# A buffer pool closed early for two more loads in flight, and the order of a first stretch dealt anew

## The chip, the cores and the metric

The kernel runs on one NeuronCore of a Trainium2 chip. A core has five engines with instruction streams of their own: TensorE (PE in the profile, its weight load is PEld), VectorE (DVE), ScalarE (ACT), GpSimd (POOL) and SyncE (SP, which here issues most DMAs). They meet through semaphores. The DMA engines move data between HBM and SBUF; matrix products are summed in PSUM. The metric is the device time of one execution in microseconds (us).

## The reference

Eight batches of block-recurrent cross attention: 512 tokens and 32 states, 8 heads of 64. Tokens read the states, states read the tokens. The two results are put in one sequence of 544 rows per batch and 512 columns (heads side by side), in all 4352 rows, and a SwiGLU layer with RMS norm follows.

```python
scores = scale * np.matmul(x, state.transpose(0, 1, 3, 2))     # 8 x 8 x 512 x 32
a = softmax(scores);   xread = np.matmul(a, state)
scores2 = scale * np.matmul(state, x.transpose(0, 1, 3, 2))    # 8 x 8 x 32 x 512
a2 = softmax(scores2); sread = np.matmul(a2, x)
x = bridge(concat([xread, sread], axis=2))                     # 4352 x 512
xn = x / sqrt(mean(x * x) + 1e-06) * rms_g
g, val = xn @ w_gate, xn @ w_val                               # 512 x 1536 each
return silu(g) * val @ w_out                                   # 1536 x 512
```

The weights arrive as 64-bit floats. The kernel reads them as 8-byte words and makes 32-bit floats of them on the chip.

## The kernel before

**Weights.** The three matrices are cut into 18 pieces of 1 MB: piece 0 is a gate piece, 1 a value piece, 2 an output piece, and so on in threes, one three for each of six blocks of the hidden layer (in the order 0, 3, 1, 4, 2, 5). A piece is loaded as raw words into one of three buffers of the pool `raws` (L241), ScalarE makes the exponent from one 16-bit part of each word in two steps, `lin` (L274) and `ex` (L277), VectorE shifts the rest (L298) and joins the two (L302). When VectorE has joined a piece, its buffer is free, and the load of the piece three further on is issued (`load_piece(k + RAW_AHEAD)`). After each value piece the block's pair of weights is stored to HBM for later batches (`w_d`, L307); they come back in `w_m` (L222).

**The work of a batch.** The tokens' read of the states is turned round: the states are multiplied with the gate and value weights first (`own_weights`, L753; ScalarE copies the result to `v`, L765), and the hidden layer is then the product of attention weights `aT_s` and `v`. For batch 0, this is done head on (L806, silu `t` L812, product `hb` L816). Its output projection is made in groups: of a 2 by 2 split of the matrices, four products per group (L1039), some with sums of `hb` or of the output weights `wo` (`group`). Four of a group's seven go one after the other into one and the same bank of PSUM (`groups_chained`, stream `p`); each time VectorE (ScalarE in the first group) adds the bank, as it then stands, to one of four sums (`chained_sums`, stream `x`, L1078 in the profile's line for the add). Three have banks of their own (`groups_direct`, `r`). From batch 1 on, the hidden layer is made with seven products of half the size for eight (L910), with sums of `aT_s` on GpSimd (`aT_t`, L828 to L830) and of `v`, and the projection likewise on two levels (L1273). For that, VectorE makes sums of the output weights once: `wt` (L1115) and `w` with further `wt` (L1227), for outer products 2, 3 and 6 during batch 0 (stream `Q`) and 0, 1, 4 and 5 during batch 1 (stream `q`). The operands `h` of the inner products are also made on VectorE (L1321 to L1327). The states' rows of all batches go through the layer at the end.

**The order.** Nothing is scheduled by a planner on the chip. The program is cut into streams of steps, each named by a letter, and strings tell which stream takes its next step: ORDER for batch 0 and the first stretch, FIRST for batch 1, PERIOD for batches 2 to 6, LAST for batch 7, STATES for the end. Each engine then runs its own instructions in that order; a wait on one holds up what stands behind it on the same engine. Letters that matter here: `e` exponents and `d` joins of the pieces, `v` own weights, `h`, `t`, `u` hidden layer of batch 0, `s` and `S` states' reads of batches 0 and 1, `w` the first steps of batch 1, `z` a product on ones that keeps TensorE awake.

**Room.** What belongs to the attention of batch 0 and to the conversion of weights lives in pools of an exit stack `early`: `raws`, `line`, `v_0`, `conv` and `x_0`, the last with the tokens of batch 0, their scores and the like. All are closed together, when the first `k` or `w` step comes.

## Time and profile before

| what | value |
|---|---|
| median of 3 runs | 735.96 us (734.49 to 736.7) |
| profiled execution | 735.84 us |
| its span in the trace | 734.1 us |
| TensorE busy | 727.0 us (99%) |
| VectorE busy | 573.6 us (78%) |
| ScalarE busy | 350.8 us (48%) |
| GpSimd busy | 287.5 us (39%) |
| granted TensorE clock, mean | 1.00 |

The span runs from the first to the last instruction of the trace; the execution's own time is 1.74 us longer. Rows of the timeline give the start in the span, the length, engine, line, operation, output and inputs, shapes and how many instructions are put together; in brackets stands the engine's idle time just before them, and what ended it. Starts and lengths are in us. Rows of the chain give the start, the length and what the end of the run hung on at that time. A 32-bit product of four matmuls in the program stands as eight in the trace.

### The profile page before, as it was taken

The page shows a single profiled execution, that of the slowest core. Times are in us where ns is not written, and L with a number is a line of the kernel's source. Part 1 is how long each engine was busy: PE and PEld are TensorE (multiplying, and loading weights), DVE is VectorE, ACT ScalarE, POOL GpSimd, SP SyncE. Part 2 cuts the span into 40 slices and gives each one's busy share as a digit, 9 for nine tenths or more (in the row PEclk, how much of TensorE's full clock was granted, in tenths as well). Part 3 has the DMA queues.
Part 4 walks back from the last instruction along what each step waited for, and adds up shares of the span by engine and source line. Part 5 has one row for each costly group of instructions (what it writes and reads, how often), then busy time and mean ns, then how long its engine had stood idle before and what let it go on. Part 6 is the DMA issues. An engine that isn't in the chain of part 4 may idle for free.

```text
span 734.1 us, 14464 instructions
## 1 busy us (share of the span) xinstructions
PE 727.0 (99%) x5676; PEld 605.3 (82%) x5676; DVE 573.6 (78%) x972; ACT 350.8 (48%) x610; POOL 287.5 (39%) x376
## 2 busy tenths in 40 slices
PE   8999999999999999999999999999999999999998
PEld 7654657789977997799888987899779987899996
DVE  5886799999848995699569984899569955888852
ACT  5987842562365336553365326533655336411220
POOL 2322037432474128512753247412851277325400
PEclk9999999999999999999999999999999999999999
DMA  8899966973692298408870588229840782063411
GB/s 234 306 327 327 335 225 213 304 303 100 212 308 68 103 325 322 114 31 306 273 249 5 213 273 318 58 99 325 325 113 32 302 277 77 1 233 113 140 48 29
DMA packets 58940, 146.17 MB, mean 199 GB/s; under 512 B 10228, under 2 KB 30200, under 8 KB 51960
## 3 DMA queue, kind: packets, MB, share of 16 engines
q1 hardware_dynamic: 47824, 126.30, 48.6%
q10 hardware_dynamic: 11048, 18.95, 8.9%
q8 instruction: 45, 0.74, 0.4%
q14 instruction: 23, 0.19, 0.1%
HBM read 116.46 MB, written 28.77 MB: 198 GB/s over the span
## 4 chain that ended last, share of the span: by engine, by line
PE 92%; DMA 3%; DVE 2%; ACT 2%; issue 0%; SPq 0%; DVEq 0%; ACTq 0%
PE f L910 40%; PE f L1273 32%; PE pv L753 4%; PE f L1039 4%; PE pv L806 3%; PE f L1135 2%; PE at L753 2%; DMA raw<-in_moe_w_val_dram 1%; PE at L456 1%; DMA raw<-in_moe_w_out_dram 1%; DMA raw<-in_moe_w_gate_dram 1%; PE f L680 1%; PE at L374 1%; ACT ex L277 1%; ACT lin L274 1%; PE at L325 0%
## 5 line engine op out<-in xcount | busy, mean ns | idle before, releaser
L910 PE MATMUL f<-aT_s,v 128*128 128x256 f32 x504 | 120.5, 382 | 0.0
L910 PEld LDWEIGHTS f<-aT_s,v 128*128 128x128 f32 x504 | 94.4, 190 | 24.6 <-issue 7.5
L1301 POOL TENSOR_TENSOR kept<-kept 128x256 f32<-128x256 f32 x28 | 20.8, 743 | 211.5 <-DVE kept L1313 147.9
L973 DVE TENSOR_TENSOR g<-g,f 128x512 f32<-128x512 f32 x84 | 56.9, 684 | 57.6 <-PE f L910 41.3
L910 PE MATMUL f<-aT_t,vs 128*128 128x256 f32 x336 | 86.5, 381 | 0.0
L1273 PE MATMUL f<-w,h 128*128 128x128 f32 x588 | 74.4, 276 | 0.0
L1273 PEld LDWEIGHTS f<-w,h 128*128 128x128 f32 x588 | 69.7, 192 | 4.1 <-DVE eB L662 4.1
L910 PEld LDWEIGHTS f<-aT_t,vs 128*128 128x128 f32 x336 | 63.0, 190 | 10.3 <-issue 1.0
L964 ACT ACTIVATE hb<-g 128x1024 f32<-128x1024 f32 x42 | 44.4, 1058 | 54.9 <-DVE g L973 54.7
L780 POOL TENSOR_TENSOR vs<-v 128x256 f32<-128x256 f32 x42 | 31.2, 744 | 81.5 <-ACT v L765 81.4
L1286 ACT COPY kept<-f 128x512 f32<-128x512 f32 (+1 forms) x56 | 29.2, 532 | 67.3 <-PE f L1273 61.8
L765 ACT COPY v<-pv 128x512 f32<-128x512 f32 x56 | 31.1, 592 | 36.7 <-PE pv L753 34.2
L973 DVE TENSOR_TENSOR c<-c,f 128x512 f32<-128x512 f32 (+1 forms) x48 | 31.3, 652 | 17.4 <-PE f L910 17.2
L986 DVE TENSOR_TENSOR hb<-hb,f 128x512 f32<-128x512 f32 (+1 forms) x48 | 31.1, 648 | 17.5 <-PE f L910 17.5
L910 PE MATMUL f<-aT_s,vs 128*128 128x256 f32 x168 | 43.1, 379 | 0.0
L910 PE MATMUL f<-aT_t,v 128*128 128x256 f32 x168 | 43.1, 379 | 0.0
L1273 PE MATMUL f<-wo,h 128*128 128x128 f32 x336 | 42.1, 275 | 0.0
L1273 PE MATMUL f<-wo,hb 128*128 128x128 f32 x336 | 42.1, 275 | 0.0
L806 PE MATMUL pv<-aT_s,v 128*128 128x512 f32 x88 | 40.4, 599 | 0.4 <-ACT v L765 0.4
L1273 PEld LDWEIGHTS f<-wo,hb 128*128 128x128 f32 x336 | 40.3, 192 | 0.4
L1273 PEld LDWEIGHTS f<-wo,h 128*128 128x128 f32 x336 | 39.8, 192 | 0.0
L986 DVE TENSOR_TENSOR hb<-hb,c 128x512 f32<-128x512 f32 (+1 forms) x48 | 33.3, 694 | 6.1 <-ACT hb L964 5.4
(261 smaller groups left out, 1632.4 us busy)
## 6 DMA issues: line engine op xcount, KB each, us to landing
w_m<-w_d SPq DMA_DIRECT2D x48, 1024.0 KB
w<-t_d SPq DMA_DIRECT2D x49, 576.0 KB
out_dram<-kept SPq DMA_DIRECT2D x30, 256.0 KB
raw<-in_moe_w_val_dram SPq DMA_DIRECT2D x6, 1024.0 KB
raw<-in_moe_w_out_dram SPq DMA_DIRECT2D x6, 1024.0 KB
w_d<-w_m SPq DMA_DIRECT2D x6, 1024.0 KB
x_b<-in_x_dram SPq DMA_DIRECT2D x6, 1024.0 KB
x_d<-xB ACTq DMA_DIRECT2D x6, 1024.0 KB
```

The source lines that it names most:

```text
L753: TE.matmul(out=pv[e][Ns * j:Ns * j + Ns, :], lhsT=stT_g[b][D * e:D * e + D, j, :], rhs=w[D * e:D * e + D, j].rearrange("p m k f -> p (m k ...
L765: SE.copy(v[:, e].rearrange("p m k f -> p (m k f)"), pv[e])
L780: GE.tensor_tensor(out=vs[:, 0], in0=a21, in1=a22, op=ALU.add)
L806: TE.matmul(out=to[0], lhsT=lhs(i, k), rhs=r, start=(i == 0), stop=(i == len(rhs) - 1))
L910: TE.matmul(out=ps[:, i, 0:half], lhsT=l[:, i, :], rhs=r, start=(start and i == 0 and k == 0), stop=(k == len(lhs) - 1), skip_group_check= ...
L964: SE.activation(out=hb[:, 2 * mp:2 * mp + 2, 0:n].rearrange("p m (c t) -> p m c t", c=2), in_=q["g"][:, :, :, 0:half], func=ACTF.Silu if s ...
L973: VE.tensor_tensor(out=to, in0=to, in1=q[ps][:, :, 0:half], op=ALU.add)
L986: VE.tensor_tensor(out=part, in0=part, in1=val, op=ALU.mult)
L1039: TE.matmul(out=bank[:, r, :], lhsT=lhs[:, k, P * r:P * r + P], rhs=rhs[:, k], start=(start and r == 0 and k == 0), stop=(stop and k == 1) ...
L1273: TE.matmul(out=to[half][:, slot, :], lhsT=lhs[:, k, :], rhs=rhs[:, k, :], start=(fresh and n in (0, 4) and k == 0), stop=(k == QM - 1), s ...
L1286: SE.copy(of_half(k, i), banks[name][i])
L1301: GE.tensor_tensor(out=k[:, 4:8:3], in0=k[:, 5:6].to_broadcast([P, 2, QD]), in1=k[:, 4:8:3], op=ALU.add)
```

## The change

The pool `x_0` moves to an exit stack of its own, `first`. A new stream `o` of one step closes it and opens in its place a pool `raws_2` with two more buffers for raw pieces, and loads pieces 11 and 12 into them. From piece 8 on, a joined piece issues the load five further on rather than three. The two strings ORDER (397 letters, now 398) and FIRST (324, as before) are dealt anew, with the same number of steps of every stream beside the one `o`; PERIOD, LAST and STATES are unchanged.

```diff
+RAW_MORE = 2
+MORE_FROM = 8
...
 ORDER = (
-    "zzzzaazaaggaaaaaziiezzeebzgaddaabbadedbbageadbbbsssbzaaeaAAassAAsbbbbsaaaaaAAbbb"
...
+    "zzzzaazagaaaaggaazzdzbzaageeeabbeabbbaadddebbsssbzaaaaAAAAessbbbAAssdabaaabbabsd"
...
 FIRST = (
-    "vxlhthtaahhqaathhvvaahhauuuxxhtqqqththhuuthhfqhqqxqaauuuhxtuuxthqqthhtuaaqhuuqqh"
...
+    "aaaahhvattvaxxxhtvhhhhhauutttuhhhxhxtaahhqqqqqauuuutfquuxqqqhqqqtthhthhhhhuxxuuu"
...
     conv = early.enter_context(tc.tile_pool(name="conv", bufs=2))
-    x_0 = early.enter_context(tc.tile_pool(name="x_0", bufs=1))
+    first = ExitStack()
+    x_0 = first.enter_context(tc.tile_pool(name="x_0", bufs=1))
...
-        raw[k] = raws.tile([P, 8 * P + 1, 4], I16, name="raw")
+        j = k - MORE_FROM - RAW_AHEAD
+        pool = more[0] if j >= 0 and j % (RAW_AHEAD + RAW_MORE) < RAW_MORE else raws
+        raw[k] = pool.tile([P, 8 * P + 1, 4], I16, name="raw")
...
+    more = []
+
+    def more_room():
+
+        first.close()
+        more.append(early.enter_context(tc.tile_pool(name="raws_2", bufs=RAW_MORE)))
+        for j in range(RAW_MORE):
+            load_piece(MORE_FROM + RAW_AHEAD + j)
+        yield
...
-                    load_piece(k + RAW_AHEAD)
+                    load_piece(k + RAW_AHEAD + (RAW_MORE if k >= MORE_FROM else 0))
...
-               "e": exponents(), "d": values(),
+               "e": exponents(), "d": values(), "o": more_room(),
```

On SyncE, in the middle of the first stretch, where the loads of raw pieces (`raw`) stand among the stores of weight pairs (`w_d`) and a load of a pair back (`w_m`), the rows before are these; the first is piece 10 of the 18, counted from 0:

```order
L241 DMA raw_646<-in_moe_w_val_dram 128x4x1024
L307 DMA w_d1_144<-w_m_574 128x2048
L241 DMA raw_700<-in_moe_w_out_dram 128x2x2048
L241 DMA raw_743<-in_moe_w_gate_dram 128x4x1024
L241 DMA raw_747<-in_moe_w_val_dram 128x4x1024
L307 DMA w_d4_147<-w_m_714 128x2048
L222 DMA w_m_770<-w_d0_143 128x2048
L241 DMA raw_776<-in_moe_w_out_dram 128x2x2048
```

And now:

```order
L246 DMA raw_637<-in_moe_w_val_dram 128x4x1024
L322 DMA w_d1_144<-w_m_601 128x2048
L246 DMA raw_721<-in_moe_w_out_dram 128x2x2048
L246 DMA raw_723<-in_moe_w_gate_dram 128x4x1024
L246 DMA raw_741<-in_moe_w_val_dram 128x4x1024
L246 DMA raw_751<-in_moe_w_out_dram 128x2x2048
L246 DMA raw_755<-in_moe_w_gate_dram 128x4x1024
L322 DMA w_d4_147<-w_m_748 128x2048
L225 DMA w_m_777<-w_d0_143 128x2048
```

Two loads of raw pieces more stand ahead of the store of the next pair. (Line numbers in the body are 15 higher in the changed kernel, a few less near its top.)

On ScalarE, at about the same place, `lin` and `ex` are the two steps of a piece's exponents, `t` a silu of batch 0's hidden layer, `kept` and `c` the first group's sums, `v` the copies of own weights. Before:

```order
L274 ACTIVATE lin<-raw,bounds 128x1024
L277 ACTIVATE ex<-lin,bounds 128x1024
L812 ACTIVATE t<-pv 128x512
L1076 COPY kept<-f 128x512
L765 COPY v<-at 128x512 x2
```

And now, where the same `kept` and `v` stand:

```order
L827 ACTIVATE t<-pv 128x512
L1091 COPY kept<-f 128x512
L780 COPY v<-at 128x512 x2
L827 ACTIVATE t<-pv 128x512
L289 ACTIVATE lin<-raw,bounds 128x1024
L292 ACTIVATE ex<-lin,bounds 128x1024
```

The read of a piece that stood ahead of `t`, `kept` and `v` now follows them, behind a further `t`.

On TensorE, at the passage from batch 0 to batch 1, the products into the one bank (f_525 before, f_496 now) of a later group, among the own weights of batch 1 (`at`, `pv` from `w_m`) and the products with banks of their own, stood so before:

```order
L753 MATMUL at_1144<-w_m_889,stT_g_708 32x512
L1039 MATMUL f_525<-wo_153,hb_154 128x256 x4
L1039 MATMUL f_650<-wo_153,group_1106 128x256 x4
L1039 MATMUL f_651<-group_962,hb_154 128x256 x4
L1039 MATMUL f_525<-group_962,group_1106 128x256 x4
L707 MATMUL at_1203<-ident_110,sr_1060 128x128
```

And now:

```order
L768 MATMUL at_1149<-w_m_918,stT_g_702 32x512
L1054 MATMUL f_496<-wo_153,hb_154 128x256 x4
L1054 MATMUL f_627<-wo_153,group_1092 128x256 x2
L722 MATMUL at_1170<-ident_110,sr_1055 128x128
L1054 MATMUL f_628<-group_955,hb_154 128x256 x2
L1054 MATMUL f_496<-group_955,group_1092 128x256 x4
L1054 MATMUL f_628<-group_955,hb_154 128x256 x2
```

Between the two products into the one bank eight matmuls stood; now four and a transpose (`at_1170`).

On VectorE, the adds from that bank (`kept` or `c22` with f_525 or f_496) stand among the sums of weights. Before:

```order
L1078 TENSOR_TENSOR kept_637<-kept_637,f_525 128x512
L1115 TENSOR_TENSOR wt_1043<-wo_153,wt_1043 128x512
L1083 TENSOR_TENSOR c22_638<-c22_638,f_649 128x512
L1227 TENSOR_TENSOR w2_1115<-wt_1043,w2_1115 128x384 x2
L1227 TENSOR_TENSOR wt_1043<-wt_1043 128x3x128
L1078 TENSOR_TENSOR c22_639<-c22_639,f_525 128x512
```

And now:

```order
L1093 TENSOR_TENSOR kept_663<-kept_663,f_496 128x512
L1242 TENSOR_TENSOR w2_1163<-wt_1007 128x384
L1242 TENSOR_TENSOR w2_1163<-wt_1007,w2_1163 128x384
L1098 TENSOR_TENSOR c22_664<-c22_664,f_626 128x512
L1242 TENSOR_TENSOR w2_1163<-wt_1007,w2_1163 128x384
L1242 TENSOR_TENSOR wt_1007<-wt_1007 128x3x128
L1093 TENSOR_TENSOR c22_665<-c22_665,f_496 128x512
```

Between the two adds from the bank one subtraction of 128x384 more stands now, and the addition to `wt` (L1115 before) has gone ahead of the first of them.

More of the change, by code (lines that the diff above doesn't have):

```diff
@@ L27 @@
 ORDER = (
-    "zzzzaazaaggaaaaaziiezzeebzgaddaabbadedbbageadbbbsssbzaaeaAAassAAsbbbbsaaaaaAAbbb"
-    "sAdAAbbAbbdaeabvedvAbbvhhhdehteeAAAeAAudddsspteviupAvSiesvsdddhteeessshhheuxdddr"
-    "vtuTTrAevTTSWveWppxeeAAAddrrWWAAAdArppxheStppeeeddddhuhtvhdWWWxuvAveeAhthudddeAs"
-    "sehthuAAdprpSAAAAATrTrxTTppeexddvvvppxAAASSSSSSerrhheedddetupWepxerhddtWdWWWhvvv"
-    "pSkkuhAthhStAAphkkkrQkkQAAAQQxuurrTTTTppQAwwwwwwwxpprrrrkcQQQxpkpQQcQxcwQwcSS"
+    "zzzzaazagaaaaggaazzdzbzaageeeabbeabbbaadddebbsssbzaaaaAAAAessbbbAAssdabaaabbabsd"
+    "AAdAAebbbbbaevvaAbvhebhhteeAAddAeupshAsdddtuvpvvesAASsshehdSSsddhehtueeedsrWtddW"
+    "vurTTAAAvvxeiiiihAeppTTrrSAxeAAAssWoSeeppxehddWrrdddddtuppxvvvhtSAAhuheedAhhhtud"
+    "eeAAtSSSruTTpTWSpxeWTArApAAWdpxrredddeWrpAedAvpAAvveexhteeehdhAAWpuddhddedvtvvWW"
+    "ukpxWShShhkkkrtuAkkkAAhQtuTpTTTrrQpxQQArppAwwwwkxwwpQQprSwwcrQQxppkcQQQSxrcwcQ"
 )
@@ L42 @@
 FIRST = (
-    "vxlhthtaahhqaathhvvaahhauuuxxhtqqqththhuuthhfqhqqxqaauuuhxtuuxthqqthhtuaaqhuuqqh"
-    "hhqqqtuuxththhtxaxuutvxhhtxkaaxhtaakkukuahhhhuuthhhuuutttauhffaahtauuuuhuhuhutaa"
-    "apphuuGuukppappppfpkkGppppacGckkkpkkkppkpppppppckgpkkakkaakaaskkkkkpkkpascsakkaa"
-    "aagpspgsagpcsaoopgkggppkcpppppppaappppsssakoppaakkpkkpksokoopafapwwsxxxwxxxcssls"
-    "fcoo"
+    "aaaahhvattvaxxxhtvhhhhhauutttuhhhxhxtaahhqqqqqauuuutfquuxqqqhqqqtthhthhhhhuxxuuu"
+    "hatthqqxuukthktkhhuutfavqhtukaaGaqhtxxxaaffhhhuuuthhhuuutuathtuaahhtsuuuhhuuhupa"
+    "pthappcapppcpGuuukkukkkkkaakkkpppkaGppppppppcpppkkgpskpkkkkppkcgpscpggaapppksscl"
+    "pgaaakaapgkssaakkkkakppakaappppsspsspppaaaooakpogpkpckkakkppaopawwxofwxxlfcooxxx"
+    "osss"
 )
```

## The prediction

> **What bounds the kernel now.** I read the engine shares first, then busy time by stretch, then TensorE's timeline around its few holes, then the chain of work that ended last. In the shares (busy us, share of the span) TensorE has almost no room.
>
> ```profile
> span 734.1 us, 14464 instructions
> PE 727.0 (99%) x5676; PEld 605.3 (82%) x5676; DVE 573.6 (78%) x972; ACT 350.8 (48%) x610; POOL 287.5 (39%) x376
> ```
>
> 734.1 − 727.0 leaves 7.1 us without a matmul. The view by stretches (length, busy time of PE, its weight load, DVE, ACT, POOL, then clock, DMA share, GB/s) splits them:
>
> ```profile
> 0.00:82.00 82.00, 78.55 (x485) 49.73 (x486) 61.17 (x114) 65.94 (x91) 21.57 (x45) 1.00 0.90 299
> 82.00:730.40 648.40, 648.40 (x5193) 555.55 (x5191) 512.41 (x859) 284.47 (x519) 265.93 (x331) 1.00 0.54 187
> 730.40:734.10 3.70, 0.02 (x1) 0.00 (x0) 0.00 (x0) 0.37 (x1) 0.00 (x0) 0.93 0.16 44
> 1.05 0.79 PE L1413 MATMUL f<-wake 128*128 128x256 f32 x1 [1.05 <-DVE wake L160]
> ```
>
> The tail of 3.7 us is the last store, which the change does not touch, and the first 1.05 us precede any matmul. That leaves 82.00 − 78.55 − 1.05 = 2.40 us of visible waiting, all of it before 82 us. From there to the last matmul TensorE never shows idle, at full granted clock. Since the change neither adds nor removes a matmul, removing waits can pay at most about these 2.4 us, which is 0.33%; and the 650 us behind them can only lose. Something near 0.3% is also what a measurement of this kernel can tell from no change.
>
> Of the visible holes (what ended each stands in the brackets) these are the first, the largest, and the products ahead of the largest and of a small one:
>
> ```profile
> 11.96 0.63 PE L528 MATMUL at<-ident,x_b 128*128 128x128 f32 x4 [0.75 <-DMA x_b<-in_x_dram]
> 65.25 1.98 PE L806 MATMUL pv<-aT_s,v 128*128 128x512 f32 x4
> 67.65 3.70 PE L806 MATMUL pv<-aT_s,v 128*128 128x512 f32 x8 [0.42 <-ACT v L765]
> 80.26 0.81 PE L1039 MATMUL f<-wo,hb 128*128 128x256 f32 x3
> 81.16 1.10 PE L1039 MATMUL f<-group 128*128 128x256 f32 x4
> ```
>
> Matmuls' ends are modelled, so idle time understates a wait; start to start is sharper. Back to back, four products of batch 0's hidden layer and eight of its projection each take 1.72 us here:
>
> ```profile
> 57.26 1.88 PE L806 MATMUL pv<-aT_s,v 128*128 128x512 f32 x4
> 58.98 1.89 PE L1039 MATMUL f<-group 128*128 128x256 f32 x8
> 60.70 3.60 PE L806 MATMUL pv<-aT_s,v 128*128 128x512 f32 x8
> ```
>
> So the hole at 67.65 costs more than its 0.42 (65.25 + 1.72 = 66.97, some 0.1 for the change of form: 0.58), and the one at 81.16 is 81.16 − 80.26 − 3 × 0.215 = 0.25. With smaller ones, an estimate of 0.2, about 1.0 us of waiting lies between the weight product at 49.09 and batch 1's at 114.07.
>
> **What the change does to the first stretch.** The chain and ScalarE's timeline show what the pieces of weights cost:
>
> ```profile
> 36.63 8.53 DMA raw<-in_moe_w_val_dram
> 47.72 1.23 DVE L302 TENSOR_TENSOR w_m<-raw,ex 128x1024 int32<-128x1024 int32 x1 [0.36 <-ACT ex L277]
> 56.08 7.52 DMA raw<-in_moe_w_out_dram
> 63.69 1.29 ACT L274 ACTIVATE lin<-raw,bounds 128x1024 f32<-128x1024 int16 x1 [1.53 <-DMA raw<-in_moe_w_out_dram]
> 66.06 0.58 ACT L812 ACTIVATE t<-pv 128x512 f32<-128x512 f32 x1
> 67.00 1.08 ACT L765 COPY v<-at 128x512 f32<-128x512 f32 x2
> 49.09 1.09 PE L753 MATMUL at<-w_m,stT_g 64*32 64x512 f32 x16
> ```
>
> The first row is piece 7, the second its words on VectorE, the third piece 11. Piece 7 lands at 45.16 and its words are put together by 48.95, when the product at 49.09 can go. Piece 11 is issued only at 56.08 (a buffer must come free), lands at 63.6, and ScalarE stands 1.53 us in front of it. Behind that read, in ScalarE's order, are the silu `t` and the two copies `v` on which TensorE waits at 67.65. This is the hole of 0.58.
>
> *Two more buffers.* SyncE's queue now issues pieces 11 and 12 as soon as the states of batch 0 are read, behind the store of `w_d[3]`, at about 49.5, and piece 13 after piece 8's last words rather than piece 10's. The issues themselves are of equal number; SyncE's row is the store, the other the stretch behind it:
>
> ```profile
> 49.39 0.50 SPq L307 DMA_DIRECT2D w_d<-w_m  x1
> 48.00:60.00 12.00, 11.99 (x62) 8.57 (x61) 11.72 (x20) 11.57 (x15) 0.00 (x0) 1.00 0.97 326
> ```
>
> The transfers have little room to come sooner: the DMA engines are 0.97 busy from 48 to 60 us. A queue that is full moves the same bytes in the same time, so I give piece 11 one to two microseconds, not the seven by which its issue moves, and only the later pieces five or more. TensorE waits for none of the later ones. The two new issues also wait for the last reader of the pool that is given up; behind them on SyncE stands only piece 13, so a late release would delay loads, and costs the path nothing up to the seven microseconds they are ahead.
>
> *ScalarE's order.* What takes the hole at 67.65 away is mostly that the new order puts `t` and `v` ahead of the read of piece 11; 0.58, 0.25 and the small ones go together. I take the whole 1.0 us. Its lower bound is nothing (rival C).
>
> *Before 49 us.* The first part of the order is dealt anew as well.
>
> ```profile
> 23.25 0.69 DVE L580 TENSOR_TENSOR eS<-aT_s,pv 128x512 f32<-128x512 f32 x1
> 23.86 1.22 DVE L302 TENSOR_TENSOR w_m<-raw,ex 128x1024 int32<-128x1024 int32 x1
> 25.14 0.37 SPq L241 DMA_DIRECT2D raw<-in_moe_w_val_dram  x1
> 35.38 1.24 DVE w_m L302
> ```
>
> The third weight product, at 49.09, hangs on piece 7, which could be issued at 36.63 when piece 4's words at 35.38 were done, and piece 4 was issued at 25.14, behind piece 1's words. In the new order VectorE has more of batch 0's state reads behind it by then, so piece 1's words are free of one such step of 0.6 us (`eS` at 23.25). An estimate is that piece 4 gains 0.5 and the third product 0.4 us, as the copies on ScalarE between them keep their lengths. It can't be more than the visible holes ahead of that product, 2.40 − 0.42 = 2.0, and a new wait of the same size, +0.4, isn't excluded either.
>
> **What it does behind 81 us.** Here nothing can be won and the question is which cover goes. Batch 0's projection runs four products per group; two of them (first and last here) go into one bank of PSUM, and VectorE must add the first to its sum before the last may write:
>
> ```profile
> 114.07 1.09 PE L753 MATMUL pv<-w_m,stT_g 64*32 64x512 f32 x16
> 115.95 1.99 PE L1039 MATMUL f<-wo,hb 128*128 128x256 f32 x8
> 117.78 1.89 PE L1039 MATMUL f<-wo,group 128*128 128x256 f32 x8
> 121.23 1.03 PE L1039 MATMUL f<-group 128*128 128x256 f32 x4
> ```
>
> The first of the two is through issuing at 115.95 + 1.72 = 117.7, the last starts at 121.23; two other products stand between, 117.78 to 121.2, 3.45 us. In the new order half of each and a transpose stand there: 8 × 0.215 + 0.11 = 1.84 us. On VectorE the add has as much in front of it as before:
>
> ```profile
> 116.07 0.67 DVE L1083 TENSOR_TENSOR c<-c,f 128x512 f32<-128x512 f32 x1
> 118.14 1.08 DVE L1227 TENSOR_TENSOR wt<-wt 128x384 f32<-128x384 f32 x1
> 119.14 0.68 DVE L1078 TENSOR_TENSOR c<-c,f 128x512 f32<-128x512 f32 x1
> 108.11 0.55 DVE L1227 TENSOR_TENSOR wt<-wt 128x384 f32<-128x384 f32 x1
> 115.68 1.06 POOL L829 TENSOR_TENSOR aT_t<-aT_s,aT_t 128x256 f32<-128x256 f32 x1
> ```
>
> That add ended at 119.8 before, with 1.4 us to spare. I take the add to end at 119.8 to 120.2 again (one subtraction more stands ahead of it, one addition of weights less), while TensorE, early by 1.4 us and with less in between, stands ready at about 119.1: a wait of about 0.75 us. The ends: nothing, if VectorE's subtractions run at 0.55 instead of 1.08 us, and 1.1 if all run slowly. I take 0.75, since GpSimd works beside them now as before. The rows themselves show that price: the same 128x384 subtraction takes 0.55 us at 108.11, and 1.08 at 118.14 while GpSimd is adding.
>
> The Trainium skill, page "SBUF — State Buffer", section "Who interferes with whom", has a rule for it: a VectorE instruction whose two inputs are both in SBUF contends with a GpSimd instruction that reads SBUF, and the loser stands still; with one SBUF input it does not. The trace agrees: `c<-c,f`, with one input in PSUM, stays at 0.67 beside GpSimd. By the rule the wait comes to 0.75 to 1.1 us; were it wrong here, to nothing. It speaks against this change, which leaves less time for those subtractions beside GpSimd.
>
> *Batch 1's hidden layer and projection.* FIRST has the same steps in a new order; the sixteen weight subtractions stand later in it. VectorE is what TensorE can come to wait for:
>
> ```profile
> 113.00:129.00 16.00, 16.00 (x110) 11.65 (x109) 15.35 (x24) 4.57 (x9) 13.74 (x14) 1.00 0.72 246
> 130.00:190.00 60.00, 60.00 (x438) 52.32 (x423) 58.72 (x102) 31.23 (x53) 17.85 (x20) 1.00 0.65 226
> 180.14 0.49 DVE L1323 TENSOR_TENSOR h<-h,hs 128x384 f32<-128x384 f32 x1
> 180.96 1.50 PE L1273 MATMUL f<-w,h 128*128 128x128 f32 x12
> ```
>
> VectorE is idle for 1.28 us of the 60, and the operand of the product at 180.96 was ready at 180.63: 0.33 us. TensorE arriving up to 1.4 us earlier, less the 0.75 it has already waited, leaves 0.65 against 0.33 here; 0 to 0.5 us of new waiting, of which I take 0.2. The period of batches 2 to 7, the last batch and the states' own layer keep their orders, so nothing is counted there.
>
> **Sum.** −0.4 (before 49) − 1.0 (49 to 114) + 0.75 (the shared bank) + 0.2 (batch 1) = −0.45 us. The profiled execution took 735.84 (0.12 under the median of 735.96, which is well within what the three runs spread over): 735.4 us.
>
> **Rivals.**
>
> *A: all holes go and no new one opens.* VectorE's subtractions are quick and the bank is free in time. 735.84 − 1.4 = 734.4. For it: the next wait is only 0.75 us, from a time walked by hand. Against: 3.45 us between the products fall to 1.84.
>
> *B, slower: VectorE becomes the bound at the passage into batch 1.* The place is 113 to 190 us. If nine of the sixteen subtractions of weights, now later, fall beside GpSimd's work, each costs 1.08 − 0.55 = 0.53 more, 4.8 us. VectorE's 0.33 of margin and 1.28 of idle take 1.6, and beyond that point each microsecond is TensorE's: +3.2. 735.84 − 1.4 + 0.75 + 3.2 = 738.4. For it: VectorE is 98% busy there (58.72 of 60), and GpSimd works for 13.74 of the 16 us at the passage. Against: from 130 on GpSimd is busy for 17.85 of 60 only.
>
> *C: the change doesn't do what it says.* The DMA engines are full, so pieces 11 and 12 land when they did; ScalarE's reads then stand where they stood, and the 1.0 us stays: 735.84 − 0.4 + 0.95 = 736.4. For it: the share of 0.97. Against: the order itself has `t` and `v` ahead of the read of piece 11.
>
> **Chances.** Forecast 0.52, A 0.16, B 0.22, C 0.10. The limits of 0.3% are 733.8 and 738.2. A passes the lower one only if it also finds most of the holes before 49 us, 0.06; B passes the upper with 0.20, the rest of it stops short. So faster 0.06, same 0.74, slower 0.20. The range is 733.9 (A with half a microsecond more) to 738.6 (B with 0.2 more), which leaves out about 2 in 10.
>
> **What would show it.** The load of piece 11 issued near 49.5 and landing at 61 to 63; batch 0's `v` ready without a hole near 67; TensorE's weight product of batch 1 near 112.7, not 114.07; a hole of about 0.75 us ahead of the second product of the shared bank near 120, ended by VectorE's add; VectorE's idle time in 130 to 190 near nothing. It would be wrong if holes of more than 1 us ahead of `h` or `hb` appear in batch 1 (B), if the third weight product waits longer than now, or if the DMA engines deliver pieces 8 to 10 later because 11 and 12 take their share.

## The result

The changed kernel takes 733.6 us (median of 9 runs, 732.23 to 734.23), the kernel before in the runs beside it 735.7 us (9 runs, 734.49 to 736.83). The ratio is 0.9969, with a 95% interval of 0.9958 to 0.9979: 2.1 us or 0.3% faster. A second measurement gave the same ratio (0.9959 to 0.9979). I had forecast 735.4 us, in a range that began at 733.9: the sign is right, the size is not, and the time lies 0.3 us outside the range.

The page of the changed kernel, engine shares first, and the three stretches cut as those of before (the middle one ends with the last matmul):

```profile
span 731.9 us, 14461 instructions
PE 725.5 (99%) x5676; PEld 605.5 (83%) x5676; DVE 575.6 (79%) x972; ACT 348.4 (48%) x608; POOL 291.4 (40%) x376
```

```profile
0.00:82.00 82.00, 79.54 (x504) 52.89 (x505) 63.51 (x116) 66.55 (x94) 25.53 (x45) 1.00 0.88 310
82.00:728.20 646.20, 645.85 (x5174) 552.66 (x5172) 512.08 (x857) 281.47 (x515) 265.91 (x331) 1.00 0.53 187
728.20:731.90 3.70, 0.07 (x1) 0.00 (x0) 0.00 (x0) 0.37 (x1) 0.00 (x0) 0.79 0.16 45
130.00:190.00 60.00, 60.00 (x424) 53.61 (x423) 59.06 (x104) 30.62 (x52) 15.63 (x18) 1.00 0.64 227
```

The span is 2.2 us shorter. TensorE's idle time went from 7.1 to 731.9 − 725.5 = 6.4 us, which is 0.7. The other 1.5 us were *busy* time before, for the same 5676 matmuls: waits that the modelled ends of matmuls had covered. My ceiling of 2.4 us, taken from visible idle time, was therefore a ceiling for the wrong thing; that the gain stays under it is chance. The last row shows that batch 1 did not get a new bound: VectorE is busier (59.06 of 60, against 58.72), and TensorE is still never idle.

The idle time of TensorE that is left in the first 130 us, gaps under 0.15 us aside, with what ended it (the last row comes after 82 us and is new):

```profile
1.05 3.78 PE L1428 MATMUL f<-wake 128*128 128x256 f32 x8 [1.05 <-DVE wake L163]
18.58 0.63 PE L570 MATMUL at<-ident,eS 128*128 128x128 f32 x4 [0.62 <-DVE stT L354]
22.97 1.05 PE L600 MATMUL f<-of_head,eS 128*128 128x4 f32 x8 [0.30 <-DVE eS L595]
47.49 1.09 PE L768 MATMUL at<-w_m,stT_g 64*32 64x512 f32 x16 [0.36 <-DVE w_m L317]
125.30 1.58 PE L768 MATMUL pv<-w_m,stT_g 64*32 64x512 f32 x16 [0.35 <-ACT v L780]
```

The holes at 67.65 (copies `v`) and 81.16 are gone, and so are those at 36.75 and 39.19 that before had between its first and third weight product. The third weight product starts at 47.49 instead of 49.09.

**An account of lost time.** Since idle time understates waits, I add up from the trace, for all matmuls in order, the distance from one start to the next, less what that shape takes back to back (the lower quartile of its distances over the whole of before: 0.215 us for 128x256, 0.43 for 128x512). What is left is time lost, including the fixed cost of going from one shape to another. Read at the same amount of finished work instead of the same time, it can be compared between kernels whose steps have another order. The four stages are: up to 22 us of work (a little behind the first weight product), 22 to 35 (to just ahead of the third), 35 to 95 (through the passage into batch 1), and the rest.

| kernel (one profile each) | to 22 | 22 to 35 | 35 to 95 | rest | ratio to before, 95% interval |
|---|---|---|---|---|---|
| before | 10.11 | 2.95 | 10.27 | 56.58 | 1 |
| changed | 8.92 | 2.19 | 9.12 | 57.53 | 0.9969 (0.9958 to 0.9979) |
| changed, second profile | 9.36 | 2.18 | 8.87 | 56.87 | 0.9969 (0.9959 to 0.9979) |
| e1_buffers_only | 11.47 | 3.20 | 8.63 | 56.70 | 0.9986 (0.9977 to 0.9995) |
| e2_orders_only | 9.18 | 2.18 | 12.53 | 57.70 | 1.0007 (0.9998 to 1.0017) |
| e5_new_start | 9.49 | 3.13 | 9.08 | 56.59 | 0.9988 (0.9978 to 0.9998) |
| e6_old_start | 9.59 | 2.16 | 9.30 | 56.63 | 0.9982 (0.9973 to 0.9991) |
| e3_old_first | 9.47 | 2.22 | 8.88 | 57.09 | 0.9982 (0.9973 to 0.9991) |
| e4_new_first | 11.56 | 3.19 | 10.04 | 56.84 | 1.0005 (0.9997 to 1.0014) |
| e7_start_buffers | 9.33 | 3.23 | 9.06 | 56.70 | 0.9980 (0.9971 to 0.9989) |
| e8_copies_first | 9.75 | 2.16 | 8.88 | 56.64 | 0.9971 (0.9960 to 0.9982) |
| e9_softmax_first | 10.24 | 3.33 | 9.71 | 56.58 | 0.9998 (0.9989 to 1.0006) |
| e10_best | 9.13 | 2.17 | 8.85 | 56.62 | 0.9963 (0.9951 to 0.9975) |
| e11_copies_first | 10.10 | 2.85 | 12.32 | 56.73 | 1.0020 (1.0011 to 1.0030) |
| e12_join_behind | 10.17 | 3.23 | 8.46 | 56.57 | 0.9995 (0.9987 to 1.0004) |
| e13_middle_only | 9.91 | 2.18 | 10.36 | 56.75 | 1.0002 (0.9993 to 1.0011) |

Two columns are worth a look before the experiments. The second is nearly a constant of the order: 2.16 to 2.22 in the eight profiles with the new order there, 2.95 to 3.33 in the seven with the old one unaltered. The first and third scatter by a microsecond among kernels that are alike there, so a single profile settles nothing in them that is smaller. In two profiles, those of e1 and e4, the first column (11.47 and 11.56) holds something else besides: the granted TensorE clock was 0.50 between 16 and 18 us, as in no other profile here. These two are left out of means of that column.

### The profile page after: what moved, and what is told of

Its sections match the earlier page's. It is cut to its first block, busy times and chain, and to the rows that moved or that the text cites. A ratio compares the mean times of both kernels' runs of the same rounds, so it can differ in the third digit from the quotient of the medians.

```text
span 731.9 us, 14461 instructions
## 1 busy us (share of the span) xinstructions
PE 725.5 (99%) x5676; PEld 605.5 (83%) x5676; DVE 575.6 (79%) x972; ACT 348.4 (48%) x608; POOL 291.4 (40%) x376
## 4 chain that ended last, share of the span: by engine, by line
PE 94%; DMA 2%; DVE 2%; ACT 1%; issue 0%; ACTq 0%; DVEq 0%
PE f L925 40%; PE f L1288 32%; PE pv L821 4%; PE pv L768 4%; PE f L1054 3%; PE f L1150 2%; PE at L768 2%; DMA out_dram<-c 1%; DMA raw<-in_moe_w_val_dram 1%; PE f L1428 1%; PE at L471 1%; PE f L695 1%; PE at L389 1%; PE pv L550 1%; ACT ex L292 0%
## 5 line engine op out<-in xcount | busy, mean ns | idle before, releaser
L796 POOL TENSOR_TENSOR vs<-vs,v 128x256 f32<-128x256 f32 x42 | 35.8, 853 | 3.3
```

The lines of the kernel that those rows point to most:

```text
L796: GE.tensor_tensor(out=vs[:, 1], in0=vs[:, 0], in1=a11, op=ALU.subtract)
```

## Experiments: buffers and orders apart

**e1_buffers_only.** The buffers and loads of the change, with the orders of before and one letter.

```diff
-    ...hhheuxdddrvtu...
+    ...hhheuxdddorvtu...
```

> The kernel before with the two more buffers alone: its own two orders, and one step that gives up the first pool and loads pieces 11 and 12 as soon as piece 7 is joined; from piece 8 on loads run five ahead. Theory 1 (the gain is made by the orders: about half ahead of the first weight product of batch 0, the rest by the places of ScalarE's steps up to 75 us): no change, 735.7 us, within 0.5, although piece 11 lands earlier; the hole at 67.65 shrinks at most by 0.5 us. Theory 2 (the gain is made by the buffers): about 734 us. Theory 3 (half of the gain is the luck of the first transfers, which landed earlier in the profile of after although issued alike): 735.7 us as well.

Measured: 734.11 us, ratio 0.9986. The interval excludes one, so theory 1 in its pure form falls: the buffers alone gain about 1 us. Where they gain it can be seen beside e4, which has the old first stretch without the buffers (its own result stands below). In both profiles the clock fell to 0.50 for a while, TensorE lost some 1.4 us more there than in before, and the transfers did not come later by as much; so each is the other's control. The clock is the third figure from the end in the first row; three rows of e1 follow, and three of e4:

```profile
16.00:18.00 2.00, 2.00 (x34) 0.82 (x33) 1.80 (x6) 0.28 (x1) 0.00 (x0) 0.50 1.04 230
51.90 0.56 SPq L246 DMA_DIRECT2D raw<-in_moe_w_out_dram  x1
64.54 1.28 ACT L289 ACTIVATE lin<-raw,bounds 128x1024 f32<-128x1024 int16 x1 [0.91 <-DMA raw<-in_moe_w_out_dram]
66.64 3.84 PE L821 MATMUL pv<-aT_s,v 128*128 128x512 f32 x8
57.49 0.37 SPq L241 DMA_DIRECT2D raw<-in_moe_w_out_dram  x1
64.57 1.27 ACT L274 ACTIVATE lin<-raw,bounds 128x1024 f32<-128x1024 int16 x1 [0.96 <-DMA raw<-in_moe_w_out_dram]
66.71 5.51 PE L806 MATMUL pv<-aT_s,v 128*128 128x512 f32 x12
```

The hole at the copies `v` is gone in both, with the buffers and without. Piece 11 was issued at 51.90 in e1 and at 57.49 in e4, 5.6 us apart, and ScalarE, which waited for it both times, read it at 64.54 and 64.57. For this piece the buffers gained nothing; the hole is gone because TensorE came later. In e7, which has the buffers, the old order here and the full clock, it is there again (below).

What the buffers do gain stands ten microseconds further on, at piece 13. The first four rows are of before, the last is of e1:

```profile
72.98 1.27 ACT L274 ACTIVATE lin<-raw,bounds 128x1024 f32<-128x1024 int16 x1 [2.06 <-DMA raw<-in_moe_w_val_dram]
75.94 0.69 DVE L816 TENSOR_TENSOR hb<-t,pv 128x512 f32<-128x512 f32 x1 [0.81 <-ACT t L812]
77.27 0.71 DVE L450 STREAM_TRANSPOSE aT_s<-eS 128x512 f32<-128x512 f32 x1
77.42 1.27 PE L456 MATMUL at<-aT_s,rows 32*64 32x512 f32 x5
71.65 1.23 ACT L289 ACTIVATE lin<-raw,bounds 128x1024 f32<-128x1024 int16 x1
```

ScalarE waits 2.06 us for the piece; the silu `t` behind it comes late, VectorE's `hb` waits 0.81 us for `t`, and behind `hb` on VectorE stands `aT_s`, ready at 77.98, for which TensorE's products from 77.42 on wait. From 60 to 75 us of work before loses 3.2 us, e9 (a wait of 1.85 us for the piece) 3.0 and e4 (2.58) 3.8. In e5 and e12 the piece landed sooner (1.11 and 0.69), and they lose 2.3. So do e1 and e7: with the buffers the piece is issued some 7 us sooner than in e4 and e5, and ScalarE doesn't wait for it.

**e2_orders_only.** Both new orders, the `o` left out, loads three ahead throughout.

> The two new orders without the buffers: the one step that gives up the pool is left out and loads run three ahead throughout. Theory 1: most of the gain stays, 733.6 to 734.2 us. Theory 2: the gain goes, 735 us or more, with holes on TensorE ended by ScalarE's copies or by weights near 60 to 85 us, where pieces 11 to 15 come later than the new order counts on. Theory 3: near 734.6 us whichever order stands at the start.

Measured: 736.16 us, ratio 1.0007. The gain is gone, as theory 2 says: without the buffers the new orders lose 3.4 us more between 35 and 95 us of work than with them (12.53 against 9.12). The holes stand where the last pieces are used:

```profile
95.83 1.09 PE L753 MATMUL at<-w_m,stT_g 64*32 64x512 f32 x16 [1.70 <-DVE w_m L302]
99.29 0.93 PE L680 MATMUL at<-x_b,e 128*32 128x64 f32 x51 [1.31 <-ACT v L765]
85.49 10.07 DMA raw<-in_moe_w_out_dram
95.64 1.46 ACT lin L274
```

The last two rows, of the chain, tell why: a piece that is issued at 85.49, when a buffer comes free, and used at 95.6 on ScalarE, with the copies `v` behind it. Near 64 us, where ScalarE's copies `v` now stand ahead of the read of piece 11 (63.15 and 65.51), TensorE has no hole: the new order closes that one without the buffers. Neither theory 1 nor theory 2 holds alone: the new order is only good with the buffers, and the buffers pay also without it.

**e5_new_start and e6_old_start.** The first has the new order for its first 93 letters only, behind it the old one, without buffers; the second is the changed kernel with the old order for its first 95 letters. Letters that the first part has used are left out of the second, and steps that it lacks (`iia` in e5) come directly behind it, so no step is lost.

```diff
 e5_new_start
-    "zzzzaazaaggaaaaaziiezzeebzg...sAdAAbbAbbdaeabvedvAbb...
+    "zzzzaazagaaaaggaazzdzbzaage...AAdAAebbbbbaeiiavdvAbb...
 e6_old_start
-    "zzzzaazagaaaaggaazzdzbzaage...AAdAAebbbbbaevvaAbvhebhh...
+    "zzzzaazaaggaaaaaziiezzeebzg...sAdAAbbAbbdaeabevvAbvhebhh...
```

> The kernel before with the new order up to the first weight product of batch 0 only (the first 93 steps), behind it the old order, no buffers, old order of batch 1. Theory 1: first weight product near 24.7 us instead of 25.7, time 734.7 us (half of the gain). Theory 2: 735.7 us. Theory 3: the first product stands where the first transfers put it, 24.7 or 25.7 us, and the median of the runs is that of before, 735.7 us.

> The changed kernel with the old order up to the first weight product of batch 0 (95 steps), all else as changed, buffers included. Theory 1: first weight product near 25.7 us, time 734.6 us (the other half of the gain stays). Theory 2: 733.6 us. Theory 3: 733.6 us, with the first product at 24.7 or 25.7 us by luck.

Measured: 0.9988 and 0.9982. The start is worth 0.12%, or 0.9 us, where it is added to before, and 0.13%, about 1 us, where it is taken from the changed kernel. That is what theory 1 forecast for it, and it speaks against theory 3, though not strongly: e5's interval just excludes one, and e6's overlaps that of the changed kernel. The first weight product began at 24.83 and 25.17 us, where 24.7 and 25.7 were expected. Luck is there all the same: the transposes of the second half's tokens, which wait for `x_b` where it lands late, begin between 10.8 and 12.0 us in the profiles, with its load issued at 4.23 to 4.25 in all of them. It strikes old and new starts alike, and it is in the first column. At equal landing the traces give the start less: 9.75 in e8 (transposes at 11.95, new start) against 10.11 in before (11.96, old), and 9.36 in the changed kernel's second profile (11.49) against 9.59 in e6 (11.51).

**e7_start_buffers.** New start and buffers, the rest of both orders old.

```diff
-    ...ssbzaaeaAAassAAs... (ORDER up to the first v: old)
+    ...ssbzaaaaAAAAessb... (ORDER up to the first v: new; one o behind piece 7's join)
```

> The kernel before with the new start (up to the first weight product) and the two buffers, but the old order of the rest and of batch 1. If the parts add: the start gave 0.12% and the buffers alone 0.14%, so a ratio of 0.9974, and the new dealing between 25 and 125 us is worth only the 0.05% that are left to the changed kernel's 0.9969. If the buffers' gain and the start's are the same waits, seen twice: 0.9986. If it is the middle of the order that uses the buffers: 0.9986 as well, with the holes near 37 and 39 us (weights, copies of v) still there.

Measured: 0.9980. The parts may add (0.9974 was worked out, the interval is 0.9971 to 0.9989, and the buffers alone had 0.9986). The difference to 0.9969, about 0.8 us, would be the new deal's behind the start; the intervals overlap, but the table's second column shows a like amount at its place, 3.23 here and 2.19 in the changed kernel. The hole at the copies `v` is here in spite of the buffers; ScalarE waited 1.44 us for piece 11, issued at 49.23 and read at 62.88, where e5 without buffers issued it at 55.40 and read it at 62.96:

```profile
66.85 3.70 PE L821 MATMUL pv<-aT_s,v 128*128 128x512 f32 x8 [0.34 <-ACT v L780]
```

**e3_old_first and e4_new_first.** Batch 1's order old in the changed kernel, and new in the kernel before.

```diff
 FIRST = (
-    "aaaahhvattvaxxxhtvhhhhhauutttuhhhxhxtaahhqqqqqauuuutfquuxqqqhqqqtthhthhhhhuxxuuu"
+    "vxlhthtaahhqaathhvvaahhauuuxxhtqqqththhuuthhfqhqqxqaauuuhxtuuxthqqthhtuaaqhuuqqh"
```

> The changed kernel with batch 1 in its old order (FIRST as before, all else as changed). Theory 4 (batch 1's new order neither pays nor costs: from its first weight product on, the time lost beside matmuls was alike in all profiles so far): 733.6 us or a ratio to before of 0.997, as the changed kernel; the small hole ahead of the third weight product of batch 1, behind ScalarE's copies of v, goes or stays at most half a microsecond. Theory 5 (the new order of batch 1 is fitted to the new end of batch 0, and pays half a microsecond or more): ratio 0.998 or above.

> The kernel before with the new order of batch 1 alone (FIRST as changed, the old first stretch, no buffers). Theory 4 (batch 1's order neither pays nor costs): ratio 1.000, within 0.0009. Theory 5 (it pays half a microsecond or more by itself): 0.999 or less. My prediction on record had it cost 0.2 us: 1.0003.

Measured: 0.9982 (0.9973 to 0.9991) and 1.0005 (0.9997 to 1.0014). By itself the new order of batch 1 gains nothing: e4 speaks for theory 4. Whether it fits the new end of batch 0 better (theory 5) these runs don't settle: e3's interval overlaps that of the changed kernel, and its profile loses about as much (77.7 us in all four columns, against 77.8 and 77.3).

## Experiments: what makes the first 48 us

**e9_softmax_first and e12_join_behind.** In before, VectorE's subtraction of the first softmax stands behind the join of piece 0, which waits for that piece to land. e9 moves the subtraction, and on ScalarE the exponential, ahead of conversion steps; e12 moves VectorE's subtraction only.

```diff
 e9_softmax_first
-    "zzzzaazaaggaaaaaziiezzeebzgaddaabb...
+    "zzzzaazaaggaaaaaziiezzbzgaaaeeddbb...
 e12_join_behind
-    "zzzzaazaaggaaaaaziiezzeebzgaddaabb...
+    "zzzzaazaaggaaaaaziiezzeebzgaaddabb...
```

> The kernel before with six instructions moved at its start and nothing else: VectorE's subtraction and ScalarE's exponential of the first softmax of batch 0 (eS) stand ahead of the conversion of piece 0 of the weights (raw and w_m on VectorE, ex and the second lin on ScalarE) instead of behind it. Theory 6 (the start's gain is this: the softmax no longer waits for the first piece to land): eS's exponential about 1.3 us sooner than the 12.60 us of before, the transposes of eS near 12.5 us, first weight product near 24.7 us, ratio 0.9985 to 0.999. Rival (the start's gain comes from the states' scores and TensorE's transposes being dealt anew): ratio 1.000, first weight product near 25.5 us.

> The kernel before with one instruction moved: VectorE's subtraction eS of the first softmax stands ahead of the first half of piece 0's conversion (raw, w_m) instead of behind it; ScalarE's order is that of before. Theory 6 again (the start's gain is that this softmax no longer stands behind piece 0's join): ScalarE's exponential near 12.0 instead of 12.6 us, the copy of xT with it, the transposes of eS 0.5 to 0.6 us closer to those of the second half's tokens (0.91 between their starts in before, 0.4 to 0.6 in the changed kernel); time lost up to the first weight product down by 0.5, ratio 0.9990 to 0.9997. Rival (something else of the new start): no change of these distances, ratio 1.000.

e9: ratio 0.9998. The exponential did come 1.1 us sooner, at 11.47, and TensorE's transposes of `eS` no sooner, at 13.91: they waited for a copy of `xT`, which stood behind the two conversion steps that I had moved (12.01 to 13.30). The run refuted its expectation and, by its own edit, not the theory. e12 is the clean one:

```profile
9.65 0.76 ACT L274 ACTIVATE lin<-raw,bounds 128x512 f32<-128x512 int16 x1 [3.05 <-DMA raw<-in_moe_w_gate_dram]
11.81 0.63 ACT L546 ACTIVATE eS<-eS 128x512 f32<-128x512 f32 x1
12.87 0.60 PE L528 MATMUL at<-ident,x_b 128*128 128x128 f32 x4
13.31 0.63 PE L555 MATMUL at<-ident,eS 128*128 128x128 f32 x4
19.41 0.63 PE L555 MATMUL at<-ident,eS 128*128 128x128 f32 x4 [0.53 <-DVE stT L339]
```

With the piece landing when it did in before (9.65, there 9.66) and the tokens too, the exponential is at 11.81 instead of 12.60, and the transposes of `eS` follow those of the tokens by 0.44 us instead of 0.91, as they do in the profiles with the new start (0.43 to 0.58). So this is a cause, and moving one instruction shows it. But the next wait takes it back: at 19.41 TensorE stands for `stT`, and by 22 us of work nothing is left (10.17 against 10.11). The ratio is 0.9995, which is not clear of one. Up to 10 us of work this one instruction is all that the new start gains at equal landing: e12 has lost 5.53 there, e8 with the whole new start 5.51, before 6.02. By 22 us of work e8 still has 0.4 of it, and e12 nothing; which of the other new steps keep it is not shown.

**e11_copies_first.** Before, with ScalarE's copies of block 1's `v` ahead of the conversion of piece 5.

```diff
-    ...AAudddsspteviupAvSiesvsdddhteee...
+    ...AAudddssptviupAvSisvesedddhteee...
```

> The kernel before with one thing moved: ScalarE's two copies of block 1's v stand ahead of the two conversion steps of piece 5 (lin, ex) instead of between and behind them. Theory 7 (between 25 and 48 us the new order's gain of 0.8 to 1.0 us is that copies of v no longer stand behind a conversion): the wait at 39.19 goes, and time lost beside matmuls between the first and the third weight product falls from 2.9 to 3.3 us, as in the five profiles with the old order there, to 2.3 to 2.5; ratio 0.999. Rival (the gain comes from TensorE having other work there, dealt anew): it stays at 3 or above, ratio 1.000.

Measured: 1.0020, the slowest of all. The expected effect is there: up to 30 us of work the kernel loses 0.8 us less behind the start than before does. Then it is paid back twice over. These are VectorE's rows, and the two products of TensorE that wait for them:

```profile
41.70 1.23 DVE L302 TENSOR_TENSOR wo<-raw,ex 128x1024 int32<-128x1024 int32 x1 [2.38 <-ACT ex L277]
45.39 0.68 DVE L816 TENSOR_TENSOR hb<-t,pv 128x512 f32<-128x512 f32 x1
48.91 1.23 DVE L302 TENSOR_TENSOR w_m<-raw,ex 128x1024 int32<-128x1024 int32 x1
46.12 1.98 PE L806 MATMUL pv<-aT_s,v 128*128 128x512 f32 x4 [0.41 <-DVE hb L816]
50.29 1.09 PE L753 MATMUL at<-w_m,stT_g 64*32 64x512 f32 x16 [1.32 <-DVE w_m L302]
```

The conversion of piece 5 on ScalarE is now later, and its join on VectorE stands where it stood: VectorE waits 2.38 us for it, with everything behind that in its order. So the copies behind a conversion were what held TensorE at 39.19; and what ScalarE gives to one, it takes from another, unless VectorE's order goes with it.

**e13_middle_only.** Before, with the whole new deal between the first and the third weight product.

```diff
-    ...daeabvedvAbbvhhhdehteeAAAeAAudddsspteviupAvSiesvsdddhteeessshhheuxdddrv...
+    ...daeabevvAbvhebhhteeAAddAeupshAsdddtuvpvvesAASsshehdSSsddhehtueeedsrWtddWvii...
```

> The kernel before with the new order between its first and its third weight product only (old start, old order behind, no buffers, old order of batch 1). Theory 7 in its wider form (the middle's gain is the deal of all engines there): time lost between the two products near 2.2 us, as in all profiles with the new order there, and kept behind them: ratio 0.9987. Rival (paid back behind, as when the copies alone were moved): lost time near 2.2 there, but more between 48 and 85 us, where a piece comes late; ratio 0.9995 to 1.001.

Measured: 1.0002, the rival's forecast. The stage loses 2.18, as in all kernels with that order, and the microsecond comes back as one hole, at once behind it:

```profile
53.55 1.78 PE L1039 MATMUL f<-wo,group 128*128 128x256 f32 x7 [1.30 <-DVE group L1033]
49.44 0.69 DVE L1033 TENSOR_TENSOR group<-group,hb 128x512 f32<-128x512 f32 x1
50.05 1.77 DVE L1033 TENSOR_TENSOR hb<-hb 128x512 f32<-128x512 f32 x1
51.74 1.75 DVE L1033 TENSOR_TENSOR group<-hb,group 128x512 f32<-128x512 f32 x1
49.48 1.79 POOL L1023 TENSOR_TENSOR wo<-wo 128x512 f32<-128x512 f32 x1
51.23 1.72 POOL L1023 TENSOR_TENSOR group<-wo,group 128x512 f32<-128x512 f32 x1
```

Here the place is one that I had not looked at, and the mechanism is the one that I had weighed elsewhere. VectorE's sums of `hb` and GpSimd's sums of `wo`, both with two operands in SBUF, fall on each other: 1.77 us instead of 0.69. In the changed kernel GpSimd has all four steps on constants (`groups`, stream `i`) ahead of its sums, which then start at 52.71, when VectorE's four are done:

```profile
50.63 0.74 DVE L1048 TENSOR_TENSOR hb<-hb 128x512 f32<-128x512 f32 x1
51.29 0.69 DVE L1048 TENSOR_TENSOR group<-hb,group 128x512 f32<-128x512 f32 x1
52.71 1.27 POOL L1038 TENSOR_TENSOR wo<-wo 128x512 f32<-128x512 f32 x1
```

In e13 and e6, which have the old start, two of the four are made there, and the sums come sooner; e6 shows the same lengthening once (1.76 us). The Trainium skill, page "SBUF — State Buffer", section "Who interferes with whom", says that the port pair which VectorE shares with GpSimd is an exclusive lock, and that a VectorE instruction with two SBUF inputs contends with a GpSimd instruction that reads SBUF. These rows agree: GpSimd's sum ends at 51.27, and VectorE's, begun at 50.05, ends 0.55 us later. The price of a collision here is 1.1 us for each of VectorE's two sums.

## Experiments: the hole that the change opened

**r_after_again** is the changed kernel once more, **e8_copies_first** has two copies moved in batch 1, **e10_best** has these and two moves on VectorE in the start.

```diff
 e8_copies_first, e10_best
 FIRST = (
-    "aaaahhvattvaxxxhtv...
+    "aaaahhvatxxtvaxhtv...
 e10_best
 ORDER = (
-    ...sssbzaaaaAAAAessbbbAAssdabaaabbabsdAAdAA...
+    ...sssbzaaaAAaAAessbbbAAssabaaabbabsddAAdAA... (and the first d of piece 1 directly ahead of its second)
```

> The changed kernel once more, unaltered, beside the next three on one chip. Its ratio to before should be 0.9969 again, within its interval (0.9958 to 0.9979). Its profile gives a second look at the start, where the landing of the first transfers differs from run to run: the first weight product between 24.4 and 25.5 us, and at the hole at 125.30, which should be there again if it isn't luck.

> The changed kernel with one thing moved: in batch 1, ScalarE's two copies of the third own weights' v stand ahead of the copy of c, which waited for a store from c's buffer, instead of behind it. If that copy is what holds the weight product up (0.35 us of idle, 0.5 from start to start at 125.30): the hole goes, and the time is 733.1 to 733.6 us, ratio 0.9962 to 0.9969. Rival: TensorE then waits at the next place, for c, and the ratio stays 0.9969; or c is needed sooner than v, 0.9975.

> The changed kernel with ScalarE's copies of v moved as in the run e8_copies_first, and on VectorE two moves at the start: the copy of stT goes ahead of the first half's eS (TensorE waits for it, 0.6 us, at 18.58), and the first step of piece 1's conversion goes behind the second half's eS (TensorE waits for that one, 0.3 us, at 22.97). If these waits are what they look like: first weight product 0.5 to 0.9 us sooner after the first transposes than in the changed kernel, ratio 0.9955 to 0.9963, better than both kernels. Rival: the first weight product is bound by piece 1's words on VectorE, whose sum of work ahead is the same, and the ratio stays at 0.9965 to 0.997.

ScalarE's rows in the changed kernel show what the hole at 125.30 hangs on, and those of e8 behind them show that it is gone:

```profile
124.17 0.59 ACT L975 COPY c<-f 128x512 f32<-128x512 f32 x1 [2.40 <-DMA out_dram<-c]
124.65 1.08 ACT L780 COPY v<-pv 128x512 f32<-128x512 f32 x2
```

```profile
123.68 1.07 ACT L780 COPY v<-pv 128x512 f32<-128x512 f32 x2 [1.35 <-PE pv L768]
124.64 0.60 ACT L975 COPY c<-f 128x512 f32<-128x512 f32 x1
125.44 1.09 PE L768 MATMUL pv<-w_m,stT_g 64*32 64x512 f32 x16
```

The copy of `c` waits until the sum that was in its buffer is stored, and the copies of `v` stood behind it. The rest of the span loses 56.64 in e8, where the changed kernel lost 57.53 in one profile and 56.87 in the other. In that other one the hole shows no idle time, and ScalarE's copy of `c` waited 1.74 us for the store instead of 2.40: its size is luck, 0.9 us or 0.2 beside e8. The first weight product of that profile began at 24.98, as expected. The ratios of the three runs are 0.9969, 0.9971 and 0.9963, and e10's median is 732.69 us, beside 733.26 for the changed kernel on the same chip. It is clearly faster than before. Its interval (0.9951 to 0.9975) overlaps the changed kernel's, so that it beats that one is likely and not shown. In its profile the wait for `stT` is down to 0.2 us lost, from 0.7 to 0.8. The first weight product began 13.33 us behind the transposes that wait for `x_b`, against 13.64 and 13.49 in the changed kernel: 0.2 to 0.3 us less, not the 0.5 to 0.9 expected.

## Why the prediction was wrong

**Before 49 us: predicted −0.4, measured −1.6 and −1.4** (the third weight product at 47.49 and 47.66 in the two profiles of the changed kernel, against 49.09). This is the step that failed. In the account, against before's 10.11 + 2.95, these profiles lost 11.11 and 11.54 up to just ahead of that product: 1.95 and 1.52 less. The means over all profiles in which the stage stands unaltered are 9.36 for the new start (seven) against 9.93 for the old one (four at the full clock), 2.18 for the new middle (eight) against 3.18 for the old one (seven); together −1.6. I had costed this part by one chain, piece 1 to piece 4 to piece 7, and looked for what was late on it. The start's share lies on another chain, softmax behind a join, with the luck of the first loads beside it, and the middle's mostly on a third, copies behind a conversion. I had the rows of both holes (13.76 and 39.19), had left them out of the working, and took their idle time for their price: 0.31 and 0.29 us, where start to start they cost 0.47 and 0.45, and more behind them.

**49 to 114 us: predicted −1.0, measured −1.15 and −1.4** (9.12 and 8.87, against 10.27). The size is near, with luck in it: the old order without the buffers lost 9.5 there in the mean of five profiles, the new order with them 9.0 in the mean of six. ScalarE's order does take away the hole at 67.65, as I had it: e2 closes it without the buffers, and e7, with the buffers and the old order, has it. What I had wrong was that TensorE would wait for none of the later pieces. What I had put down as "smaller ones", 0.2 us in all, includes 0.6 us at 77.42, where the trace of before shows no idle time. These matmuls wait for `aT_s`, and through it for piece 13; the same matmul has a visible wait of 0.73 us in e11, with `aT_s` named. This wait, and the 0.25 at 81.16 that comes and goes with it, is what the buffers take away in the old order.

**The shared bank: predicted +0.75, measured nothing.** VectorE's add and the product behind it in the changed kernel:

```profile
116.58 0.67 DVE L1093 TENSOR_TENSOR c<-c,f 128x512 f32<-128x512 f32 x1
117.38 1.93 PE L1054 MATMUL f<-group 128*128 128x256 f32 x8
113.03 0.55 DVE L1242 TENSOR_TENSOR w<-wt 128x384 f32<-128x384 f32 x1
113.62 0.97 DVE L1242 TENSOR_TENSOR w<-wt,w 128x384 f32<-128x384 f32 x1
115.11 0.55 DVE L1242 TENSOR_TENSOR w<-wt,w 128x384 f32<-128x384 f32 x1
115.58 1.08 DVE L1242 TENSOR_TENSOR wt<-wt 128x384 f32<-128x384 f32 x1
110.70 1.22 DVE L484 TENSOR_TENSOR aT_s<-aT_s,at 128x1024 f32<-128x1024 f32 x1
```

The bank is free at 117.25, and the product starts at 117.38, directly behind the one ahead of it. The cover did shrink as worked out; a margin of 0.13 us is left. My working had a slip besides: 117.7 − 1.4 + 1.84 makes TensorE ready at 118.1, not 119.1, so by its own terms the wait should have been 1.7 to 2.1 us. What failed is that I kept VectorE on its old clock, and moved TensorE only. VectorE's own passage (the last row) came 2.9 us sooner than the 113.57 of before, more than TensorE's 2.2. GpSimd worked without a pause beside them, and of the four subtractions two were lengthened, to 0.97 and 1.08, and two were not: the price that I had put on all of them fell on half.

**Batch 1: predicted +0.2, measured nothing at the place named, and a wait elsewhere.** The projection's products in 130 to 190 us had no hole. The 0.35 us of idle time at 125.30, for ScalarE's copies behind a copy that waited for a store, I had not foreseen; start to start it makes nearly all of the 0.95 us more that the rest of the first profile loses.

**The rivals.** A (all holes go, 734.4) was nearest: the bank was free in time and the holes before 49 us went as well, but it had counted that stage at 0.4 only. The columns of the first profile make −1.95 − 1.15 + 0.95 for the rest = −2.15, which is the difference of the spans (they must add up to it). B did not come about: VectorE is 0.34 us busier in 130 to 190, and TensorE loses nothing there. C is refuted by the order: nothing waits at 67. Its premise was right for piece 11, which e1 and e7 issued some 6 us sooner than e4 and e5 and read at the same time; in the changed kernel it was issued at 48.38.

**What stays open.** How much the start is worth (0.9 us by the runs, 0.2 to 0.4 by the traces at equal landing), which of its further steps keep what e12 lost again at 19.41, whether batch 1's new order helps the new end of batch 0, and why a piece lands sooner in one run than in another: without the buffers the old order lost between 8.46 and 10.27 in the third column.

## What to carry to other kernels

On an engine that is 99% busy, idle time is no ceiling for what waits cost: compare start to start by shape, at equal work, and both the price and the place of a wait change. A step moved ahead on one engine is worth only what the next engine's order lets through; the single moves at the start and at the copies here were paid back within some 20 us, once with interest, while the whole deal, with the buffers it counts on, kept its gain. Look at the granted clock of each stretch before two profiles are compared: where TensorE alone has come later, a hole closes that no change has closed. When everything up to a place comes sooner, move all engines in the working, not only the one that waits.

## Not expected of the hardware

- A 128x512 sum of two SBUF operands on VectorE took 1.77 us instead of 0.69 when it fell on a like sum on GpSimd, which in turn took 1.79 instead of 1.27.
- A load issued 5.6 us sooner (51.90 in e1, 57.49 in e4) could be read 0.03 us sooner, and one issued 6.2 us sooner (e7 and e5) 0.08 us; two pieces later the same buffers saved a wait of up to 2.58 us.
- A DMA share near one was not a fixed rate: from 48 to 60 us before moved 326 GB/s at a share of 0.97, the changed kernel 380 at 0.98; from 60 to 72 us before moved 303 at 0.91 and e1 399 at 1.03.
- In two of 16 profiles the granted TensorE clock was 0.50 between 16 and 18 us, which cost some 1.4 us; these executions (735.95 and 737.55 us) were the longest of their kernels.
- The first loads of a run land over 1 us apart from run to run, though issued within 0.02 us of one another: ScalarE, waiting for piece 0, read it at 8.45 us in e1 and at 9.66 in before.
